# The second feed-forward layer computed row by row: gelu values as weights, w2 in quarters as moving operand

## The chip, the cores and the metric

One core of a Trainium2 chip runs one program. The metric is the device time of one execution in microseconds (us), lower is better. The kernel before takes 1184.27 us in the median of three runs (1183.27 to 1184.52). All tensors are bfloat16; matmuls accumulate in float32 in PSUM.

## The reference

A transformer block with the normalisation in front: attention with 32 heads of 32, then a feed-forward layer with gelu. There are 2048 rows of 1024 values; the hidden width is 3584.

```python
def _A_ref(x, wqkv, wo):
    B, S, D = x.shape
    H = 32; Dh = D // H
    qkv = (x @ wqkv).reshape(B, S, 3, H, Dh).transpose(2, 0, 3, 1, 4)
    q, k, v = qkv[0], qkv[1], qkv[2]
    scores = jnp.einsum("bhqd,bhkd->bhqk", q, k) * Dh ** -0.5
    o = jnp.einsum("bhqk,bhkd->bhqd", _softmax(scores, axis=-1), v)
    return o.transpose(0, 2, 1, 3).reshape(B, S, D) @ wo

def _B_ref(x, w1, b1, w2, b2):
    h = _gelu(jnp.einsum("bsd,df->bsf", x, w1) + b1)
    return jnp.einsum("bsf,fd->bsd", h, w2) + b2

h = x + _A_ref(_layernorm(x), wqkv, wo)
out = h + _B_ref(_layernorm(h), w1, b1, w2, b2)
```

## The kernel before

**A written-out order.** The program has no loop on the chip. A planner (`Plan`) records each instruction with an estimated cost and with what it reads and writes, works out the semaphore waits, and keeps for every engine one list in order. Within an engine nothing is reordered later, and a waiting instruction holds up all that stands behind it on its engine. SP issues all loads and stores, in one list too.

**Chunks.** The rows go in four chunks of 512 (`CH`). Attention is worked through in 512 units `u` (four chunks, eight groups `g` of four heads, two halves of 256 queries, eight pairs of key tiles). Each unit makes scores of four heads with 8 matmuls whose weights have 32 rows (`qk`, L1131), two exponentials of 128x1024 on ScalarE (L1140), and later the matmuls with the values and the row sums (`pv`, L1216). The scores use six PSUM banks as three pairs, bank 6 takes the values' sums, and bank 7 is the only bank (`fbanks.items = [7]`) for all other matmuls of that stage.

**Filler.** All that isn't attention is written as generators that stop (`yield Need(...)`) before each step, and the planner puts steps between scores and values when TensorE has room: first the projections of keys, queries and values (`fill0`), then, beside attention of chunk `c`, the output projection, normalisation and feed-forward of chunk `c - 1` (`ffn(ci, False)`). The test for room is `t + turn + step <= due`, where `step` is the cost of one matmul step of 512 columns, `due` is 220 ns after the scores' banks are expected to be free, and `turn` is 95 ns if scores came just before. Filler matmuls there go as quads: `wide(..., quad=True)` makes four matmuls with 32 columns of weights each, at four column positions of the array, which the array does side by side. The planner counts a quad as its columns/2.4 + 2.5 ns, and 105 ns more where the kind of matmul changes (`kind`: "R" for scores, "C" for quads and values, "F" for whole-width ones).

**The feed-forward part of `ffn`.** After `hnT` (the normalised rows, transposed) the first layer makes 28 groups `fc` of 128 hidden units; each is 8 matmuls of 512 columns, an eviction, and gelu. While attention runs, gelu is a chain of VectorE steps and a tanh on ScalarE (L1460 to L1463, two groups at a time); in the tail it is one ScalarE instruction (L1445). The results stand in `gT`, hidden units by rows. The second layer takes 8 blocks `db` of 128 output columns: weights are `w2` (128 hidden by 128 output columns), the moving operand is `gT` with 512 rows, so 28 matmuls of 512 columns make a block of the *transposed* result. VectorE (L1488), in the tail ScalarE (L1485), adds `b2`, one value for each partition, on the way into `oT`. After four blocks, four transposes for each tile of 128 rows turn the result back (`transposes`, L506 as quads, L511 whole), VectorE adds the residual rows `hch` (L1495) and the store is put on SP.

**Loads of weights.** `w1` has two slots of 512 KB (`load_w1`), `w2` two slots of 896 KB (`load_w2`, one block each, asked for one block ahead; the first two are asked for six groups before the first layer's end). `hnT`, and later `oT`, stand at `hn_off`; `x3` and later the output staging `ost` at `x3_off`.

**The tail.** After the last exponential the chunk 3 (`ffn(3, True)`) runs with nothing beside it: whole-width matmuls (`tiled[0] = False`), eight banks once the filler of chunk 2 is done, six slots for `w1` and three for `w2` in the space of the keys and values.

Of the kernel before, what the change touches and what calls it, by code (L numbers as in the profile page):

```python
# [7 lines left out]
dt = mybir.dt  # L8
# [5 lines left out]
P = 128  # L14
# [221 lines left out]
def build_kernel(nc, A_x, A_wqkv, A_wo, B_w1, B_b1, B_w2, B_b2, out):  # L236
# [100 lines left out]
    ones_pp, (B_ones,) = sb("ones_pp", [P, P], dt.bfloat16)  # L337
    ones32, (B_ones32,) = sb("ones32", [P, 32], dt.bfloat16)
    blk, (B_blk,) = sb("blk", [P, 32], dt.bfloat16)
    b2bf, (Bf_b2bf,) = sb("b2bf", [P, DC], dt.bfloat16)  # L340
    b2f, (Bf_b2f,) = sb("b2f", [P, DC], dt.float32)
    b1bf, (Bf_b1bf,) = sb("b1bf", [P, FC], dt.bfloat16)
    b1f, (Bf_b1f,) = sb("b1f", [P, FC], dt.float32)
    biasm, _ = sb("biasm", [P, G, NCH], dt.float32)
# [584 lines left out]
    with_b = [("b1", b1bf, B_b1, Bf_b1bf), ("b2", b2bf, B_b2, Bf_b2bf)]  # L929
    for _, t_, src, B_ in with_b:  # L930
        dma(t_[:], src.rearrange("(c p) -> p c", p=P), 8192, writes=[B_], lanes=lanes_a, noncontig=True)
    pool(lambda g: g.tensor_copy(b1f[:], b1bf[:]), reads=[Bf_b1bf], writes=[Bf_b1f])
    pool(lambda g: g.tensor_copy(b2f[:], b2bf[:]), reads=[Bf_b2bf], writes=[Bf_b2f])


    PT, B_PTf = sb("PT", [P, NPU, 4, 512], dt.bfloat16, nbufs(NPU * 2), at=late_off)
# [320 lines left out]
    def ffn_alloc():  # L1257
        cursor[0] = region0
        f = ffn_bufs

        def area(name, nbytes):
            f[name] = cursor[0]
            cursor[0] += nbytes

        area("g_off", FC * 1024)
        area("hn_off", DC * 1024)
        area("x3_off", 4 * 2048)
        f["w1"], f["B_w1"] = sb("w1", [P, 2, DC, 256], dt.bfloat16, nbufs(2))
        f["w2_off"] = cursor[0]
        f["w2"], f["B_w2"] = sb("w2", [P, 2, FC, P], dt.bfloat16, nbufs(2))  # L1270
# [46 lines left out]
    def ffn(ci, tail):  # L1317
# [82 lines left out]
        def load_w2(db):  # L1400
            if db in w2s or db >= DC:
                return
            s = w2s[db] = n12[1] % len(B_w2_)
            n12[1] += 1
            dma(w2[:, s, :, :], B_w2[:, db * P:(db + 1) * P].rearrange("(c p) d -> p c d", p=P), FC * P * P * 2,
                writes=[B_w2_[s]], lanes=lanes_w)
# [26 lines left out]
        for bk in range(FC // 2):  # L1433
            s = w1s[bk]
            for u in range(2):
                fc = bk * 2 + u
                if u == 1:
                    load_w1(bk + len(B_w1_) - 1)
                if fc == FC - 6:
                    for db in range(len(B_w2_)):  # L1440
                        load_w2(db)
# [24 lines left out]
                yield from group([(w1[:, s, dc, u * P:(u + 1) * P], hnT[:, dc, 0:w]) for dc in range(DC)], evac,  # L1466
                                 lambda i, s=s: [B_w1_[s]] + B_hnT[:n4], n=w)
        oT, B_oT = sb(f"oT{ci}", [P, DC, 512], dt.bfloat16, nbufs(DC), at=hn_at)
        ost, B_ost = sb(f"ost{ci}", [P, 8, 512], dt.bfloat16, nbufs(8), at=x3_at)
        for hf in range(2):  # L1470
            for d4 in range(4):
                db = hf * 4 + d4
                s = w2s[db]
                bank = fbanks.next()
                quad = tiled[0]
                for fc in range(FC):
                    if fc == 6:
                        load_w2(db + len(B_w2_) - 1)
                    if fc % 2 == 0:
                        yield Need([B_gT[fc], B_gT[fc + 1], B_w2_[s]], [B_ps[bank]] if fc == 0 else [],  # L1480
                                   [g_ch[fc + 1]] if fc + 1 in g_ch else [])
                    wide(bank, 0, w, w2[:, s, fc, :], gT[:, fc, 0:w], fc == 0, fc == FC - 1,
                         [B_gT[fc], B_w2_[s]], [B_ps[bank]] if fc in (0, FC - 1) else [], fc == FC - 1, quad)
                if tail:
                    act(lambda a, bank=bank, db=db: a.activation(oT[:, db, 0:w], ps[:, bank, 0:w], ACT.Identity, bias=b2f[:, db:db + 1], scale=1.0),  # L1485
                        reads=[B_ps[bank], Bf_b2f], writes=[B_oT[db]], cost=180 + .85 * w)
                else:
                    dve(lambda v, bank=bank, db=db: v.tensor_scalar(oT[:, db, 0:w], ps[:, bank, 0:w], b2f[:, db:db + 1], None, ALU.add),  # L1488
                        reads=[B_ps[bank], Bf_b2f], writes=[B_oT[db]], cost=690)
            for t4 in range(n4):  # L1490
                bank = fbanks.next()
                yield Need(B_oT[hf * 4:hf * 4 + 4], [B_ps[bank]])
                tp = transposes(lambda k, t4=t4, hf=hf: oT[:, hf * 4 + k, t4 * P:(t4 + 1) * P], B_oT[hf * 4:hf * 4 + 4], bank, 4)
                o = hf * 4 + t4
                dve(lambda v, tp=tp, o=o, t4=t4, hf=hf: v.tensor_tensor(ost[:, o, :], tp, hch[:, t4, hf * 512:(hf + 1) * 512], ALU.add),  # L1495
                    reads=[B_ps[bank], B_hch[2 * t4 + hf]], writes=[B_ost[o]], cost=690)
                r0_ = q0 + t4 * P

                def store(r0_=r0_, hf=hf, o=o):
                    dma(out2[r0_:r0_ + P, hf * 512:(hf + 1) * 512], ost[:, o, :], 131072, reads=[B_ost[o]], lanes=lanes_o, is_out=True)  # L1500
                    if ci < NCH - 2:
                        load_rows(r0_ + 512, o % 4, hf)
# [12 lines left out]
    u = 0  # L1515
# [197 lines left out]
```

## Time and profile before

| what | value |
|---|---|
| runs | 1184.27 us median of 3 (1183.27 to 1184.52) |
| the profiled execution | 1182.17 us |
| its span, from first to last instruction | 1180.4 us |
| granted TensorE clock, mean | 0.994 |
| exponentials of attention (L1140) | 1024, 954.1 us busy, 1124 ns each |
| second layer beside attention (L529, gT and w) | 2688 matmuls of 128x512 = 672 quads, 169.0 us busy |
| second layer in the tail (L524, gT and w_t) | 224 matmuls of 128x512, 48.7 us busy |
| transposes back (L506; L511 in the tail) | 384 matmuls, 9.6 us busy; 32, 2.1 us |
| evictions with b2 (L1488 VectorE; L1485 ScalarE) | 24 of 750 ns; 8 of 687 ns |
| residual additions (L1495 VectorE) | 32 of 425 ns |
| eviction with addition from a whole bank (L1358 VectorE) | 32 of 692 ns |
| loads of w2, 896 KB: issue to landing, median | 5.9 us beside attention, 5.0 us in the tail |
| loads of w1, 512 KB | 3.7 us |

The span begins with the first instruction and ends with the last; the profiled execution's time holds some 1.8 us more around it. In rows of the timeline the columns are: start in us from the span's start, duration in us from the first start to the last end, engine, line, operation, output and inputs, weights' rows*columns and the shape, how many, and in brackets idle time before the first and what ended it. PE is TensorE, PEld its weight loads, DVE VectorE, ACT ScalarE, SPq the DMA queue of SyncE. Instructions of one engine overlap in their pipelines, so the step from start to start is shorter than the duration of one, and an engine that is "busy" throughout can still be fed late.

### The profile page before, as it was taken

What the parts mean: (1) busy time and instruction counts of PE and PEld (TensorE: products, weight loads), DVE (VectorE), ACT (ScalarE), POOL (GpSimd) and SP (SyncE); (2) the same over time, 40 slices, a digit from 0 to 9 for tenths busy, and PEclk for the clock granted to TensorE, in tenths of its full rate; (3) what the DMA queues carried; (4) which work ended last, traced back from release to release, by engine and by line L of the source; (5) the groups of instructions that cost most, each with busy time, mean ns of one, the idle gap of its engine ahead of it and who ended that gap; (6) DMA issues with size and microseconds to landing.
All of it is one profiled execution on the core that took longest, in us unless ns stands there. A gap on an engine that the chain in (4) does not pass through costs nothing.

```text
span 1180.4 us, 48866 instructions
## 1 busy us (share of the span) xinstructions
PE 1102.0 (93%) x22638; PEld 556.3 (47%) x22638; DVE 663.0 (56%) x1182; ACT 1050.8 (89%) x1157; POOL 20.1 (2%) x60
## 2 busy tenths in 40 slices
PE   6999999999998999999998999999999999997998
PEld 3646455554444444444444444444444444443443
DVE  8564565555656778444556887444667864452000
ACT  7798999899999999999999999999999999962410
POOL 2100000000000000000000000000000000000000
PEclk9999999999999999999999999999999999998999
DMA  9201000003401233442502242351012513342643
GB/s 268 46 21 39 21 3 12 12 12 92 100 12 56 84 106 77 96 101 62 144 11 74 74 127 65 79 132 57 21 56 75 153 34 96 83 145 77 177 94 99
DMA packets 231870, 91.24 MB, mean 77 GB/s; under 512 B 155376, under 2 KB 229104, under 8 KB 231664
## 3 DMA queue, kind: packets, MB, share of 16 engines
q1 hardware_dynamic: 231664, 88.10, 28.5%
q8 instruction: 177, 2.90, 1.0%
q14 instruction: 29, 0.24, 0.1%
HBM read 83.90 MB, written 4.19 MB: 75 GB/s over the span
## 4 chain that ended last, share of the span: by engine, by line
ACT 43%; PE 41%; issue 8%; DVE 5%; DMA 2%; SPq 1%; POOL 0%; POOLq 0%; DVEq 0%; ACTq 0%
ACT PT L1140 40%; PE ps L529 18%; PE ps L524 10%; PE ps L1216 6%; PE ps L1131 5%; ACT tm L1462 2%; DMA w<-in_B_w_dram 1%; PE ps L803 1%; DVE lnst L481 1%; PE ps L858 1%; DVE Rg L1229 1%; DVE gT L1448 1%; DVE QT L1231 1%; SPq L288 1%; PE ps L511 1%
## 5 line engine op out<-in xcount | busy, mean ns | idle before, releaser
L1140 ACT ACTIVATE PT<-ps 128x1024 bf16<-128x1024 f32 x1024 | 954.1, 1124 | 15.1 <-DVE biasm L681 9.7
L1216 PE MATMUL ps<-PT,V 128*32 128x256 bf16 x4096 | 227.6, 274 | 17.2 <-ACT PT L1140 11.0
L1165 DVE TENSOR_TENSOR FS<-PT 128x1024 bf16<-128x1024 bf16 x227 | 155.6, 689 | 147.3 <-ACT PT L1140 118.3
L1131 PE MATMUL ps<-QT,KT 32*128 32x256 bf16 x4096 | 203.6, 273 | 22.8 <-ACT PT L1140 18.9
L529 PE MATMUL ps<-hnT,w 128*32 128x512 bf16 x2688 | 173.0, 381 | 6.5 <-DVE gT L1448 3.9
L529 PE MATMUL ps<-gT,w 128*32 128x512 bf16 x2688 | 169.0, 380 | 0.4 <-DVE oT L1488 0.3
L1131 PEld LDWEIGHTS ps<-QT,KT 32*128 32x128 bf16 x4096 | 61.0, 92 | 196.4 <-ACT PT L1140 184.9
L1216 PE MATMUL ps<-PT,ones 128*32 128x256 bf16 x2280 | 144.0, 273 | 0.0
L1216 PEld LDWEIGHTS ps<-PT,V 128*32 128x32 bf16 x4096 | 106.2, 96 | 70.8 <-ACT PT L1140 25.2
L529 PEld LDWEIGHTS ps<-hnT,w 128*32 128x32 bf16 x2688 | 61.4, 96 | 78.0 <-issue 28.4
L1448 DVE TENSOR_SCALAR gT<-ps,b1f 128x512 bf16<-128x512 f32 x84 | 63.0, 750 | 54.9 <-PE ps L529 54.0
L529 PEld LDWEIGHTS ps<-gT,w 128*32 128x32 bf16 x2688 | 68.7, 97 | 51.5 <-issue 4.8
L1495 DVE TENSOR_TENSOR ost<-ps,hch 128x512 bf16<-128x512 bf16 x32 | 13.0, 422 | 116.5 <-PE ps L511 102.1
L1216 PEld LDWEIGHTS ps<-PT,ones 128*32 128x32 bf16 x2280 | 61.4, 97 | 10.4
L1216 PE MATMUL ps<-FS,ones 128*32 128x256 bf16 x908 | 65.2, 277 | 0.0
L529 PE MATMUL ps<-xnTe,wk 128*32 128x512 bf16 x832 | 55.6, 389 | 4.3 <-DVE kmax L646 2.3
L1463 DVE SCALAR_TENSOR_TENSOR gT<-tm,gT 128x1024 bf16<-128x1024 bf16 x42 | 51.2, 1219 | 2.7 <-ACT tm L1462 2.1
L524 PE MATMUL ps<-hnT,w_t 128*128 128x512 bf16 x224 | 50.8, 392 | 1.2 <-ACT hnT L1422 1.2
L1461 DVE SCALAR_TENSOR_TENSOR tm<-tm,gT 128x1024 bf16<-128x1024 bf16 x42 | 51.3, 1221 | 0.8
L1462 ACT ACTIVATE tm<-tm 128x1024 bf16<-128x1024 bf16 x42 | 50.3, 1197 | 0.0
L524 PE MATMUL ps<-gT,w_t 128*128 128x512 bf16 x224 | 48.7, 379 | 0.0
L1445 ACT ACTIVATE gT<-ps,b1f 128x512 bf16<-128x512 f32 x28 | 19.2, 687 | 32.5 <-PE ps L524 32.5
(135 smaller groups left out, 899.4 us busy)
## 6 DMA issues: line engine op xcount, KB each, us to landing
w<-in_B_w_dram SPq DMA_DIRECT2D x42, 512.0 KB, 3.7
w<-in_B_w_dram SPq DMA_DIRECT2D x24, 896.0 KB, 5.9
w_t<-in_B_w_dram SPq DMA_DIRECT2D x14, 512.0 KB, 3.7
w_t<-in_B_w_dram SPq DMA_DIRECT2D x8, 896.0 KB, 5.0
xr<-in_A_x_dram SPq DMA_DIRECT2D x16, 256.0 KB, 6.0
wk<-in_A_wqkv_dram SPq DMA_DIRECT2D x16, 256.0 KB, 3.1
wq<-in_A_wqkv_dram SPq DMA_DIRECT2D x16, 256.0 KB, 4.2
out_dram<-ost SPq DMA_DIRECT2D x32, 128.0 KB, 2.3
```

The lines of the kernel that those rows point to most:

```text
L524: pe(lambda p: p.matmul(ps[:, bank, lo:lo + n], lhsT, rhs, start=start, stop=stop), reads=reads, writes=writes, inc=inc, cost=mm(n))
L529: pe(lambda p, r=r: p.matmul(ps[32 * r:32 * r + 32, bank, lo:lo + n], lhsT[:, 32 * r:32 * r + 32], rhs, start=start, stop=stop, tile_posit ...
L1131: pe(lambda p, k=k, kt=kt, r=r, b=b: p.matmul(ps[:, b, k * 256:(k + 1) * 256], KT[32 * r:32 * r + 32, g, kt * P:(kt + 1) * P], QT[32 * r:3 ...
L1140: act(lambda a, safe, i=i, b=b: a.activation(PT[:, o_, 2 * i:2 * i + 2, :], ps[:, b:b + 2, :], ACT.Exp, bias=0.0 if safe else biasm[:, g, ...
L1165: dve(lambda v: v.tensor_tensor(FS[:, f_, :, :], PT[:, o_, :, 0:256], PT[:, o_, :, 256:512], ALU.add), reads=B_PT[o_], writes=[B_FS[f_]], ...
L1216: pe(lambda p, d=d, r=r, lhsT=lhsT, rhs=rhs, n=n: p.matmul(ps[32 * r:32 * r + 32, OD, d * 256:(d + 1) * 256], lhsT, rhs, start=(start and ...
L1445: act(lambda a: a.activation(gT[:, fc, 0:w], ps[:, bank, 0:w], ACT.Gelu_apprx_tanh, bias=b1f[:, fc:fc + 1], scale=1.0), reads=[B_ps[bank], ...
L1448: dve(lambda v: v.tensor_scalar(gT[:, fc, 0:w], ps[:, bank, 0:w], b1f[:, fc:fc + 1], 0.5, ALU.add, ALU.mult), reads=[B_ps[bank], Bf_b1f], ...
L1461: (E.DVE, lambda v: v.scalar_tensor_tensor(t_, t_, GB, x_, ALU.add, ALU.mult), [Bt] + Bx, [Bt], 1220),
L1462: (E.Activation, lambda a: a.activation(t_, t_, ACT.Tanh, scale=GK), [Bt], [Bt], 946),
L1463: (E.DVE, lambda v: v.scalar_tensor_tensor(x_, t_, 1.0, x_, ALU.add, ALU.mult), [Bt] + Bx, Bx, 1220)])
L1495: dve(lambda v, tp=tp, o=o, t4=t4, hf=hf: v.tensor_tensor(ost[:, o, :], tp, hch[:, t4, hf * 512:(hf + 1) * 512], ALU.add), reads=[B_ps[ban ...
```

## The change

The operands of the second layer change places. For each quarter `q` of 256 output columns and each tile of 128 rows, 28 matmuls take `gT` (128 hidden units by 128 rows) as weights and a quarter of `w2` (128 hidden by 256 columns) as moving operand, so that rows of the result come out untransposed. Two tiles share a PSUM bank. After the 28 comes one more matmul which adds `b2`: its weights are four rows, of which only row `q` is one, and its moving operand is `b2` as four rows of 256. One VectorE addition of the residual takes the whole bank to `ost`, and one store takes two tiles by 256 columns to memory. `oT`, its evictions, the transposes back and the column-wise `b2` go.

`w2` is loaded by quarters, each as two loads of 14 groups of 128 hidden units (two of 896 KB, rows of 256 values in place of 128). Quarter 0 is asked for where the first two blocks were, quarter 1 when the first layer has been recorded, quarters 2 and 3 when the quarter two before has been. Even quarters use the place of the old two slots, odd ones the place of `hnT` and of most of `w1`; `x3_off` moves in front of `hn_off` so that those lie side by side. In the tail both places are in the space of the values, `w1` has four slots in place of six, and `x3` and `hnT` move into the space of the keys.

```diff
-    b2bf, (Bf_b2bf,) = sb("b2bf", [P, DC], dt.bfloat16)
-    b2f, (Bf_b2f,) = sb("b2f", [P, DC], dt.float32)
+    b2row, (B_b2row,) = sb("b2row", [4, 256], dt.bfloat16)
...
+    dma(b2row[:], B_b2.rearrange("(a c) -> a c", a=4), 2048, writes=[B_b2row], lanes=lanes_a)
...
-        area("hn_off", DC * 1024)
         area("x3_off", 4 * 2048)
+        area("hn_off", DC * 1024)
+        f["w1_off"] = cursor[0]
...
-            f["w1"], f["B_w1"] = sb("w1_t", [P, 6, DC, 256], dt.bfloat16, nbufs(6), at=k2_off)
-            f["w2"], f["B_w2"] = sb("w2_t", [P, 3, FC, P], dt.bfloat16, nbufs(3), at=v_off)
+            f["w1"], f["B_w1"] = sb("w1_t", [P, 4, DC, 256], dt.bfloat16, nbufs(4), at=k2_off)
...
+        def load_w2(q, part=None):
+            if q not in w2s:
+                at = (v_off + q % 2 * 14336 if tail else f["hn_off"] if q % 2 else f["w2_off"])
+                w2s[q] = sb(f"w2_{ci}_{q}", [P, 2, FC // 2, 256], dt.bfloat16, nbufs(2), at=at)
+            w2, B = w2s[q]
+            for h in range(2):
+                if part in (None, h):
+                    dma(w2[:, h, :, :], B_w2[h * FC * 64:(h + 1) * FC * 64, q * 256:(q + 1) * 256].rearrange("(c p) d -> p c d", p=P), FC * P * 256,
+                        writes=[B[h]], lanes=lanes_w)
...
-        for hf in range(2):
-            for d4 in range(4):
-                db = hf * 4 + d4
...
-                    wide(bank, 0, w, w2[:, s, fc, :], gT[:, fc, 0:w], fc == 0, fc == FC - 1,
-                         [B_gT[fc], B_w2_[s]], [B_ps[bank]] if fc in (0, FC - 1) else [], fc == FC - 1, quad)
...
+        load_w2(1)
+        for q in range(4):
+            w2, B_w2_ = w2s[q]
+            for t in range(0, n4, 2):
+                bank = fbanks.next()
+                quad = tiled[0]
+                for u in range(2):
+                    lo = (t + u) * P
+                    for fc in range(FC):
+                        if fc % 2 == 0:
+                            yield Need([B_gT[fc], B_gT[fc + 1], B_w2_[fc // (FC // 2)]], [B_ps[bank]] if u == 0 and fc == 0 else [],
+                                       [g_ch[fc + 1]] if fc + 1 in g_ch else [])
+                        wide(bank, u * 256, 256, gT[:, fc, lo:lo + P], w2[:, fc // (FC // 2), fc % (FC // 2), :], fc == 0, False,
+                             [B_gT[fc], B_w2_[fc // (FC // 2)]], [B_ps[bank]] if fc == 0 else [], False, quad)
+                    wide(bank, u * 256, 256, ident[0:4, q:q + 1].to_broadcast([4, P]), b2row[:], False, True,
+                         [B_ident, B_b2row], [B_ps[bank]], True, quad)
+                o = q * 2 + t // 2
+                dve(lambda v, o=o, t=t, q=q, bank=bank: v.tensor_tensor(
+                    ost[:, o, :, :], ps[:, bank, :].rearrange("p (u c) -> p u c", u=2), hch[:, t:t + 2, q * 256:(q + 1) * 256], ALU.add),
+                    reads=[B_ps[bank]] + [B_hch[2 * (t + u) + q // 2] for u in range(2)], writes=[B_ost[o]], cost=690)
...
+                def store(r0_=r0_, q=q, o=o, t=t):
+                    dma(out2[r0_:r0_ + 2 * P, q * 256:(q + 1) * 256].rearrange("(u p) c -> p u c", p=P), ost[:, o, :, :], 131072,
+                        reads=[B_ost[o]], lanes=lanes_o, is_out=True)
...
+            if q < 2:
+                load_w2(q + 2)
```

More of the change, by code (lines that the diff above doesn't have):

```diff
@@ L928, in build_kernel @@
     v_left = [proj_v(2 * p, 0, "act") for p in range(NT // 2) if ("V", p) in jobs]
-    with_b = [("b1", b1bf, B_b1, Bf_b1bf), ("b2", b2bf, B_b2, Bf_b2bf)]
-    for _, t_, src, B_ in with_b:
-        dma(t_[:], src.rearrange("(c p) -> p c", p=P), 8192, writes=[B_], lanes=lanes_a, noncontig=True)
+    dma(b1bf[:], B_b1.rearrange("(c p) -> p c", p=P), 8192, writes=[Bf_b1bf], lanes=lanes_a, noncontig=True)
+    dma(b2row[:], B_b2.rearrange("(a c) -> a c", a=4), 2048, writes=[B_b2row], lanes=lanes_a)
     pool(lambda g: g.tensor_copy(b1f[:], b1bf[:]), reads=[Bf_b1bf], writes=[Bf_b1f])
-    pool(lambda g: g.tensor_copy(b2f[:], b2bf[:]), reads=[Bf_b2bf], writes=[Bf_b2f])
     PT, B_PTf = sb("PT", [P, NPU, 4, 512], dt.bfloat16, nbufs(NPU * 2), at=late_off)
@@ L1265, in ffn_alloc @@
         area("g_off", FC * 1024)
+        area("x3_off", 4 * 2048)
         area("hn_off", DC * 1024)
-        area("x3_off", 4 * 2048)
+        f["w1_off"] = cursor[0]
         f["w1"], f["B_w1"] = sb("w1", [P, 2, DC, 256], dt.bfloat16, nbufs(2))
         f["w2_off"] = cursor[0]
-        f["w2"], f["B_w2"] = sb("w2", [P, 2, FC, P], dt.bfloat16, nbufs(2))
+        f["w2"], f["B_w2"] = sb("w2", [P, 2, FC // 2, 256], dt.bfloat16, nbufs(2))
         f["NG"] = 3
@@ L1325, in ffn @@
         if tail:
-            f["w1"], f["B_w1"] = sb("w1_t", [P, 6, DC, 256], dt.bfloat16, nbufs(6), at=k2_off)
-            f["w2"], f["B_w2"] = sb("w2_t", [P, 3, FC, P], dt.bfloat16, nbufs(3), at=v_off)
-        w1, w2, tm = f["w1"], f["w2"], f["tm"]
+            f["w1"], f["B_w1"] = sb("w1_t", [P, 4, DC, 256], dt.bfloat16, nbufs(4), at=k2_off)
+        w1, tm = f["w1"], f["tm"]
         B_tm_ = f["B_tm"]
-        B_w1_, B_w2_, NG = f["B_w1"], f["B_w2"], f["NG"]
-        hc_at, x3_at, hn_at = (qt_off, k2_off + 24576, v_off + 21504) if tail else (hch_off, f["x3_off"], f["hn_off"])
+        B_w1_, NG = f["B_w1"], f["NG"]
+        hc_at, x3_at, hn_at = (qt_off, k2_off + 16384, k2_off + 24576) if tail else (hch_off, f["x3_off"], f["hn_off"])
         n12 = [0, 0] if tail else f["n12"]
@@ L1398, in load_w1 @@
                 writes=[B_w1_[s]], lanes=lanes_w)
[L1400 to L1406, printed above, removed]
+        def load_w2(q, part=None):
[7 more added lines that the diff above has]
+                        writes=[B[h]], lanes=lanes_w)
         for bk in range(len(B_w1_)):
@@ L1439, in ffn @@
                 if fc == FC - 6:
-                    for db in range(len(B_w2_)):
-                        load_w2(db)
+                    load_w2(0)
                 def evac(bank, fc=fc):
@@ L1467, in ffn @@
                                  lambda i, s=s: [B_w1_[s]] + B_hnT[:n4], n=w)
-        oT, B_oT = sb(f"oT{ci}", [P, DC, 512], dt.bfloat16, nbufs(DC), at=hn_at)
-        ost, B_ost = sb(f"ost{ci}", [P, 8, 512], dt.bfloat16, nbufs(8), at=x3_at)
-        for hf in range(2):
-            for d4 in range(4):
-                db = hf * 4 + d4
-                s = w2s[db]
+        ost, B_ost = sb(f"ost{ci}", [P, 8, 2, 256], dt.bfloat16, nbufs(8), at=x3_at)
+        load_w2(1)
+        for q in range(4):
+            w2, B_w2_ = w2s[q]
+            for t in range(0, n4, 2):
@@ L1474, in ffn @@
                 bank = fbanks.next()
                 quad = tiled[0]
[L1476 to L1481, printed above, removed]
-                    wide(bank, 0, w, w2[:, s, fc, :], gT[:, fc, 0:w], fc == 0, fc == FC - 1,
-                         [B_gT[fc], B_w2_[s]], [B_ps[bank]] if fc in (0, FC - 1) else [], fc == FC - 1, quad)
@@ L1484, in ffn @@
[L1484 to L1502, printed above, removed]
-                stores.append(chain([("call", store, [B_ost[o]], [], 0)]))
+                for u in range(2):
[8 more added lines that the diff above has]
+                         [B_ident, B_b2row], [B_ps[bank]], True, quad)
@@ new lines, in ffn @@
+                o = q * 2 + t // 2
+                dve(lambda v, o=o, t=t, q=q, bank=bank: v.tensor_tensor(
+                    ost[:, o, :, :], ps[:, bank, :].rearrange("p (u c) -> p u c", u=2), hch[:, t:t + 2, q * 256:(q + 1) * 256], ALU.add),
+                    reads=[B_ps[bank]] + [B_hch[2 * (t + u) + q // 2] for u in range(2)], writes=[B_ost[o]], cost=690)
+                r0_ = q0 + t * P
+                def store(r0_=r0_, q=q, o=o, t=t):
+                    dma(out2[r0_:r0_ + 2 * P, q * 256:(q + 1) * 256].rearrange("(u p) c -> p u c", p=P), ost[:, o, :, :], 131072,
+                        reads=[B_ost[o]], lanes=lanes_o, is_out=True)
+                    if ci < NCH - 2 and q % 2:
+                        for u in range(2):
+                            load_rows(r0_ + 512 + u * P, t + u, q // 2)
@@ L1504, in ffn @@
+                stores.append(chain([("call", store, [B_ost[o]], [], 0)]))
+            if q < 2:
+                load_w2(q + 2)
+        if not tail:
+            for k, q in ((0, 3), (1, 2)):
+                lo, B = (f["w1_off"], B_w1_) if q == 3 else (f["w2_off"], f["B_w2"])
+                plan.track(lo, lo + (8192 if q == 3 else 14336), B)
         marks.add(("ffn", ci))
```

## The prediction

> **What bounds the kernel now.** I read the page first: the span, the engine shares and the forty slices.
>
> ```profile
> span 1180.4 us, 48866 instructions
> PE 1102.0 (93%) x22638; PEld 556.3 (47%) x22638; DVE 663.0 (56%) x1182; ACT 1050.8 (89%) x1157; POOL 20.1 (2%) x60
> ...
> PE   6999999999998999999998999999999999997998
> ...
> ACT  7798999899999999999999999999999999962410
> ...
> ACT 43%; PE 41%; issue 8%; DVE 5%; DMA 2%; SPq 1%; POOL 0%; POOLq 0%; DVEq 0%; ACTq 0%
> ```
>
> The reader is to see two regimes. Up to slice 35 ScalarE and TensorE are both full (attention, with the feed-forward of the chunk before as filler); then ScalarE empties and TensorE alone carries the tail, the fourth chunk. So a price has to be asked twice: what does it do to ScalarE's row of exponentials, and what to TensorE's row in the tail? ScalarE first, in the timeline of its engine:
>
> ```profile
> 819.36 43.19 ACT L1140 ACTIVATE PT<-ps 128x1024 bf16<-128x1024 f32 x47
> ...
> 956.88 93.08 ACT L1140 ACTIVATE PT<-ps 128x1024 bf16<-128x1024 f32 x100
> ...
> 959.82 4.73 ACT L1140 ACTIVATE PT<-ps 128x1024 bf16<-128x1024 f32 x5
> ```
>
> One exponential lasts 1.124 us (page), but they overlap. The five at 959.82 follow each other at (4.73 - 1.124)/4 = 0.902 us: the rate of an undisturbed ScalarE. The hundred from 956.88, beside the second layer of chunk 2, need (93.08 - 1.124)/99 = 0.929; the 47 from 819.36, beside the output projection, whose filler steps are single quads of 512 columns, 0.915. So "busy" hides some 0.027 x 99 = 2.7 us of lateness in a second-layer stage: scores that come late hold ScalarE up, and TensorE's order decides it. Then TensorE:
>
> ```profile
> 96.12 1.93 PE L529 MATMUL ps<-wv,xnTl 128*32 128x256 bf16 x64
> ...
> 1034.10 0.40 PE L1131 MATMUL ps<-QT,KT 32*128 32x256 bf16 x8
> 1034.42 1.91 PE L529 MATMUL ps<-gT,w 128*32 128x512 bf16 x32
> 1036.27 0.40 PE L1131 MATMUL ps<-QT,KT 32*128 32x256 bf16 x8
> ...
> 45.41 1.91 PE L858 MATMUL ps<-wv,xnTl 128*128 128x256 bf16 x16
> 47.25 0.40 PE L830 MATMUL ps<-sqk,blk 128*32 128x512 bf16 x4
> 47.58 1.92 PE L858 MATMUL ps<-wv,xnTl 128*128 128x256 bf16 x16
> ```
>
> Four matmuls of 32 columns of weights go side by side as a quad. Eight quads of 512 in 1.91 us, less the last one's 0.379 and 0.012 between its four starts: 0.217 us each. Sixteen quads of 256 in 1.93: (1.93 - 0.273 - 0.012)/15 = 0.110. Whole-width matmuls of 256: (1.91 - 0.273)/15 = 0.109. The third and fourth rows show the price of changing the division of the array: the last 512-quad starts at 1034.42 + 7 x 0.217 = 1035.94, the scores 0.33 later instead of 0.217; back again the second score quad starts at 1034.22, the next filler 0.20 later instead of 0.11. So 0.1 us each way, 0.2 for a visit. The last three rows say the same of whole width against quads (47.05 to 47.25, 47.47 to 47.58). Last the tail:
>
> ```profile
> 1124.24 24.34 PE L524 MATMUL ps<-gT,w_t 128*128 128x512 bf16 x112
> ...
> 1149.35 1.07 PE L511 MATMUL ps<-ident,oT 128*128 128x128 bf16 x16 [0.78 <-ACT oT L1485]
> ...
> 1150.26 24.34 PE L524 MATMUL ps<-gT,w_t 128*128 128x512 bf16 x112
> ...
> 1174.63 0.69 ACT L1485 ACTIVATE oT<-ps,b2f 128x512 bf16<-128x512 f32 x1 [5.36 <-PE ps L524]
> 1175.37 0.90 PEld L511 LDWEIGHTS ps<-ident,oT 128*128 128x128 bf16 x16 [1.27 <-ACT oT L1485]
> ...
> 1175.81 1.42 DVE L1495 TENSOR_TENSOR ost<-ps,hch 128x512 bf16<-128x512 bf16 x4 [24.60 <-PE ps L511]
> 1176.26 2.22 SPq L288 DMA_DIRECT2D out_dram<-ost  x4
> ```
>
> Matmuls of 512 run at (24.34 - 0.380)/111 = 0.216 us; between the halves, and after the second, an eviction, transposes and additions stand bare.
>
> **The tail, term by term.** (1) 448 matmuls of 256 at 0.1091 replace 224 of 512 at 0.2159: 48.88 - 48.36 = +0.5 us. The doubled weight loads (98 ns) hide, as in the L858 rows, which load 128x128 weights before each 256. (2) 16 bias matmuls at 0.109: +1.7. (3) The gap between the halves goes: the next matmul could have started at 1148.42 and did at 1150.26: -1.8. (4) The end: from the last matmul's end (1174.60) to the span's end at 1180.37 were 5.8 us. Now follow one addition of 128x512 from PSUM (0.69 by the L1358 rows, the same shape), a hop of 0.06, and one store: 1.7 (the shortest landing) to 2.3 (the median), say 1.9, and about 0.45 to the end as before: 3.1, so -2.7; the last matmul is 0.1 shorter, -0.1. Without anything else: -2.4. (5) Does a bias matmul, of four rows, cost a change of division? No row of the trace has fewer than 32 rows. Below: nothing, for quads of 32 columns stay quads of 32 columns. Above: a visit each, 16 x 0.2 = 3.2, less the way back of the last, 3.1. I take the upper: the scores, whose weights have 32 rows, do pay, and a matmul's division seems to be taken from its operands' rows and columns. Tail: **+0.7 us**.
>
> The Trainium skill, TensorEngine Tiling (Array Packing), Key Properties, says that changing the tiling mode drains TensorE, while changing the tile does not. By it four rows belong to a 32-row mode, and the tail is the +0.7; read so that four rows stay in the 128-row mode it is -2.4. The rows above agree with the drain at 0.1 us a side for 32 rows; none shows four.
>
> **The attention stage.** TensorE per chunk: 448 x 0.110 - 224 x 0.217 = +0.7 us, 16 bias quads +1.8, their visits 0 to +3.2, eight transposes gone (16 matmuls at 0.056 a quad, 0.23 each) -1.8; and 8 handovers of the only filler bank in place of 16. At worst +3.9 a chunk, 11.7 for three. As mere work this is hidden: the last second-layer matmul starts at 1041.6, the exponentials end at 1049.98, and from 1066 to 1070 in the tail TensorE does nothing; with the cover gone, each us would lengthen the tail by one. VectorE's 8 evictions of 0.75 and 8 additions of 0.425 become 8 of 0.69: -3.9 us a chunk on an engine 56% busy, nothing. What is not hidden is lateness of scores, in two opposite terms.
> (6) The planner tests room for one quad of 512 but then records a pair of them, 0.43 us; a pair of 256 is 0.22 and fits the test. If the second layer's exponentials come at the 0.915 of the projection instead of 0.929, over some 100 in each of three stages: -4.2; below that nothing, since TensorE may simply use the time otherwise. I take half, **-2.1**.
> (7) The planner books a bias quad without a visit (its kind is "C", like its neighbours), so real scores come up to 0.2 later than planned, 48 times: 0 to 48 x 0.2 = +9.6. Some of it is eaten: TensorE waits for ScalarE before scores 56 times for 18.9 us (view of waits), 0.3 each, spread over the whole program, and every second bias quad is followed by a bank handover, in which TensorE waits anyway. I take a third, **+3.2**.
> (8) Gelu: the last pair is ready at 957.25 + 1.23 = 958.5, the first pass began at 953.11 and reached that pair near 961. At half the columns it gets there near 956.3 and pauses 2.2 us a chunk; the pending values are taken first. Filler, not scores: 0, at worst 3 x 2.2 in the cover above.
> (9) DMA. Quarters are loaded as two of 896 KB; such loads land after 5.9 us (in the tail 5.0). Quarter 1 lies over hnT and w1 and so is asked for at the end of the first layer, needed a quarter later (22 us as filler, 12.7 in the tail); quarters 2 and 3 wait on SP for the end of the quarter two before. Two in a row: 10 to 12 us, hidden; 12.7 - 10.0 leaves 2.7 in the tail. Behind these waits on SP stand only stores of a finished pair, whose eight slots no one takes again in the chunk, and in chunks 0 and 1 rows for the next. The tail's w1 goes from six slots to four: still three blocks of 3.45 us ahead of a landing of 3.7.
>
> Sum: +0.7 - 2.1 + 3.2 = **+1.8 us**. The profiled execution took 1182.17 us around its span of 1180.4, so 1184.0 there; the runs' median is 1184.27, and I give the forecast on it: **1186.1**.
>
> **Rivals.** (A) The forecast, 0.44; its own range, from terms 6 and 7, 1183.5 to 1190. (B) Four rows cost no visit: tail -2.4, filler -2.1, -4.5: **1179.8**. For it: the quads' columns stay; against: what the 32-row scores pay. 0.22. (C) Nothing absorbs the visits and the finer steps bring nothing: each bias quad pushes the next scores out by 0.2: +9.6 + 0.7: **1194.6**. For it: TensorE is at 9 in every slice; against: its waits for ScalarE. 0.19. (D) Visits are paid but absorbed, the finer steps bring all: -4.2 + 0.7: **1180.8**. For it: 0.915 beside single quads; against: that stage has other filler. 0.15. Slower begins for certain where term 7 exceeds term 6 by 1.7.
>
> Less than 0.2% (2.4 us) can't be told from no change here. Faster: 0.20 of B, 0.10 of D: 0.30. Slower: C's 0.18 and 0.24 of A's upper part: 0.42. Same: 0.28. The range 1180 to 1192 leaves out the far ends of B and C, about 0.2.
>
> **What would show it.** The bias rows: 0.2 us more than 0.11 from their neighbours (A, C, D) or not (B). The mean step of exponentials beside the second layer: above 0.929 C, near it A, 0.915 D. The tail from the second layer's first matmul to the end: 56.8 us with visits, 53.7 without, where it was 56.1. Wrong altogether would be a wait for w2 in the tail, or second-layer work left after the last exponential.

## The result and the profile after

The changed kernel takes 1200.48 us in the median of four runs (1198.61 to 1203.81); the kernel before took 1183.77 (1182.13 to 1184.52) beside it. The ratio is 1.0145, with a 95% interval of 1.0126 to 1.0164: the change costs 16 to 17 us. Forecast were 1186.1, with 1192 as the upper end. The page of the changed kernel:

```profile
span 1196.8 us, 54116 instructions
...
PE 1116.4 (93%) x25263; PEld 642.4 (54%) x25274; DVE 666.9 (56%) x1175; ACT 1047.3 (88%) x1149; POOL 20.3 (2%) x59
...
PE   6999999999998999999999999989899999998998
...
ACT  7798999899999999999999999999999999962400
...
q8 instruction: 198, 3.24, 1.1%
...
L1137 ACT ACTIVATE PT<-ps 128x1024 bf16<-128x1024 f32 x1024 | 955.6, 1110 | 27.9 <-PE ps L1128 16.6
...
L528 PE MATMUL ps<-w,gT 128*32 128x256 bf16 x5376 | 178.6, 273 | 5.4 <-issue 4.9
```

The span grew by 16.4 us. VectorE lost its evictions into `oT`, but its busy time went from 663.0 to 666.9 us: the planner now gives it 244 sums of exponentials of 689 ns (L1162) where it had 227. Three things are new. ScalarE's idle time before exponentials (L1137, which was L1140) is 27.9 us, of which 16.6 end with late scores. In the kernel before it was 15.1 and 3.8, by the page and by the view of waits:

```profile
L1140 ACT ACTIVATE PT<-ps 128x1024 bf16<-128x1024 f32 x1024 | 954.1, 1124 | 15.1 <-DVE biasm L681 9.7
...
ACT PT L1140 <- PE ps L1131: 3.8, 6, 1.2
```

The second layer's matmuls (L528, which was L529) have idle time that ends in "issue": TensorE stood with nothing to wait for that the trace shows. And the program has 5250 more instructions; the queue that brings instructions (q8) made 198 packets where it made 177.

Where in the span? The last exponential ends at 1065.43, before at 1049.97: attention lost 15.5 us, the tail 1.0 (131.4 after 130.4). Not all of the 15.5 stands beside the second layer, whose first matmul starts at 463.21 before and at 466.66 after. The exponentials around these two points, the same ones of each program:

```profile
461.24 5.76 ACT L1140 ACTIVATE PT<-ps 128x1024 bf16<-128x1024 f32 x6
464.69 5.64 ACT L1137 ACTIVATE PT<-ps 128x1024 bf16<-128x1024 f32 x6
```

So 3.45 us had been lost before any matmul of the second layer ran. From 52 to 463 us the granted clock was 1.00 in the kernel before and 0.98 in this execution of the changed one; it was 1.00 in both beside the second layer. The other 12.0 us are lost from there on, and ScalarE's timeline shows their form. This is the changed kernel beside the second layer of chunk 2:

```profile
972.02 23.95 ACT L1137 ACTIVATE PT<-ps 128x1024 bf16<-128x1024 f32 x26 [0.83 <-PE ps L1128]
997.15 25.83 ACT L1137 ACTIVATE PT<-ps 128x1024 bf16<-128x1024 f32 x28 [1.19 <-PE ps L1128]
1024.23 14.79 ACT L1137 ACTIVATE PT<-ps 128x1024 bf16<-128x1024 f32 x16 [1.25 <-PE ps L1128]
1039.30 14.84 ACT L1137 ACTIVATE PT<-ps 128x1024 bf16<-128x1024 f32 x16 [0.27 <-PE ps L1128]
1054.29 11.14 ACT L1137 ACTIVATE PT<-ps 128x1024 bf16<-128x1024 f32 x12 [0.15 <-PE ps L1128]
```

Within a row the step is good: (25.83 - 1.110)/27 = 0.916 us, better than the 0.929 of before. The rows are cut by gaps, the longest of 1.19 and 1.25 us; over all 98 the step is (1065.43 - 972.02 - 1.110)/97 = 0.952. It is not a steady slowing but some events. The view of TensorE's waits in the changed kernel has them (engine, line and releaser; then total us, times, longest):

```profile
PE ps L528 <- issue: 4.9, 5, 1.6
...
PE ps L1213 <- issue: 3.5, 2, 2.4
...
PE ps L1128 <- issue: 1.2, 1, 1.2
```

These are 9.6 us beside attention, in eight halts; the kernel before has no such row for TensorE. TensorE's timeline around one of them:

```profile
498.04 0.40 PE L1128 MATMUL ps<-QT,KT 32*128 32x256 bf16 x8
...
498.70 0.49 PE L528 MATMUL ps<-w,gT 128*32 128x256 bf16 x10
500.59 1.05 PE L528 MATMUL ps<-w,gT 128*32 128x256 bf16 x30 [1.39 <-issue]
501.57 0.40 PE L1128 MATMUL ps<-QT,KT 32*128 32x256 bf16 x8
```

A run of quads, all of whose operands have long been there, breaks off after ten matmuls, in the middle of the third quad, and goes on 1.39 us later. The scores behind it come 3.5 us after the scores before, and an exponential is late by it. The large halts begin at 499.2, 521.8, 758.7, 785.4, 995.3 and 1022.6 us: two in each of the three chunks, each 6 to 8 us after the first load of a pair of w2 loads was issued. The trace's DMA records beside the first:

```
instruction packets (q8, 16 KB each), start:  486.51  490.78  498.09  501.90  505.75
the two w2 loads, issue to landing:           490.96 to 496.22,  491.37 to 499.23
TensorE stands:                               499.20 to 500.59
```

A packet of 16 KB is due every 4 us here. While the two loads run, none starts for 7.3 us, and at the end of that gap TensorE stands. The size fits: by the page (3.24 + 0.24 MB)/54116 is 64 bytes for an instruction, so a packet holds some 256; a quad of 256 columns is eight instructions (four weight loads, four matmuls) in 0.110 us, and at that rate a packet lasts 3.5 us. This suggested a theory: **a pair of loads back to back keeps the instruction packets waiting, and halved matmuls eat up the instructions in hand before the next arrives.** Its rivals: the visits of the bias rows push the scores (rival C of the prediction), and the halved matmuls alone are at fault, whatever is loaded.

### The profile page after: what moved, and what is told of

It reads as the page before. It is cut to its first block, busy times and chain, and to the rows that moved or that the text cites. A ratio compares the mean times of both kernels' runs of the same rounds, so it can differ in the third digit from the quotient of the medians.

```text
span 1196.8 us, 54116 instructions
## 1 busy us (share of the span) xinstructions
PE 1116.4 (93%) x25263; PEld 642.4 (54%) x25274; DVE 666.9 (56%) x1175; ACT 1047.3 (88%) x1149; POOL 20.3 (2%) x59
## 3 DMA queue, kind: packets, MB, share of 16 engines
q8 instruction: 198, 3.24, 1.1%
## 4 chain that ended last, share of the span: by engine, by line
ACT 45%; PE 40%; issue 9%; DVE 5%; DMA 0%; POOL 0%; POOLq 0%; ACTq 0%; DVEq 0%
ACT PT L1137 41%; PE ps L528 16%; PE ps L523 10%; PE ps L1213 7%; PE ps L1128 5%; ACT tm L1460 3%; DVE lnst L480 1%; PE ps L802 1%; DVE Rg L1226 1%; DVE Rg L1224 1%; PE ps L857 1%; DVE QT L1228 1%; PE ps L510 0%; DVE gT L1446 0%; DVE gT L1461 0%
## 5 line engine op out<-in xcount | busy, mean ns | idle before, releaser
L1137 ACT ACTIVATE PT<-ps 128x1024 bf16<-128x1024 f32 x1024 | 955.6, 1110 | 27.9 <-PE ps L1128 16.6
L1162 DVE TENSOR_TENSOR FS<-PT 128x1024 bf16<-128x1024 bf16 x244 | 167.2, 689 | 160.9 <-ACT PT L1137 127.6
L528 PE MATMUL ps<-w,gT 128*32 128x256 bf16 x5376 | 178.6, 273 | 5.4 <-issue 4.9
L528 PE MATMUL ps<-hnT,w 128*32 128x512 bf16 x2688 | 173.3, 381 | 5.5 <-DVE gT L1446 4.0
L528 PEld LDWEIGHTS ps<-w,gT 128*32 128x32 bf16 x5376 | 135.7, 97 | 26.4 <-issue 18.6
L1213 PE MATMUL ps<-PT,ones 128*32 128x256 bf16 x2144 | 137.1, 274 | 0.0
L528 PEld LDWEIGHTS ps<-hnT,w 128*32 128x32 bf16 x2688 | 61.6, 96 | 76.7 <-issue 27.5
L1484 DVE TENSOR_TENSOR ost<-ps,hch 128x512 bf16<-128x512 f32 x32 | 22.1, 690 | 123.1 <-PE ps L523 100.6
L1213 PE MATMUL ps<-FS,ones 128*32 128x256 bf16 x976 | 70.1, 277 | 0.3 <-DVE FS L1162 0.2
L1213 PEld LDWEIGHTS ps<-PT,ones 128*32 128x32 bf16 x2144 | 57.7, 97 | 10.9
L528 PE MATMUL ps<-xnTe,wk 128*32 128x512 bf16 x832 | 57.3, 399 | 4.3 <-DVE kmax L645 2.3
L523 PE MATMUL ps<-w,gT 128*128 128x256 bf16 x448 | 51.7, 273 | 0.0
L1460 ACT ACTIVATE tm<-tm 128x1024 bf16<-128x1024 bf16 x42 | 50.1, 1192 | 0.0
```

The source lines that it names most:

```text
L523: pe(lambda p: p.matmul(ps[:, bank, lo:lo + n], lhsT, rhs, start=start, stop=stop), reads=reads, writes=writes, inc=inc, cost=mm(n))
L528: pe(lambda p, r=r: p.matmul(ps[32 * r:32 * r + 32, bank, lo:lo + n], lhsT[:, 32 * r:32 * r + 32], rhs, start=start, stop=stop, tile_posit ...
L1137: act(lambda a, safe, i=i, b=b: a.activation(PT[:, o_, 2 * i:2 * i + 2, :], ps[:, b:b + 2, :], ACT.Exp, bias=0.0 if safe else biasm[:, g, ...
L1162: dve(lambda v: v.tensor_tensor(FS[:, f_, :, :], PT[:, o_, :, 0:256], PT[:, o_, :, 256:512], ALU.add), reads=B_PT[o_], writes=[B_FS[f_]], ...
L1213: pe(lambda p, d=d, r=r, lhsT=lhsT, rhs=rhs, n=n: p.matmul(ps[32 * r:32 * r + 32, OD, d * 256:(d + 1) * 256], lhsT, rhs, start=(start and ...
L1484: dve(lambda v, o=o, t=t, q=q, bank=bank: v.tensor_tensor(ost[:, o, :, :], ps[:, bank, :].rearrange("p (u c) -> p u c", u=2), hch[:, t:t + ...
```

## The experiments

In the table "last exp" is the end of the last exponential, "tail" what follows it to the span's end, and "issue" the idle time of TensorE beside attention that ends in "issue", from the view of waits; all in us from the profiled execution. "From" is the start of the first matmul of the second layer beside attention; up to there TensorE has the same work in all of them. The ratio is to the kernel before on the same chip.

| kernel | median us | ratio, 95% interval | from | last exp | tail | issue |
|---|---|---|---|---|---|---|
| before | 1181.80 to 1183.77 | 1 | 463.21 | 1049.97 | 130.4 | 0 |
| after | 1200.48 | 1.0145 [1.0126, 1.0164] | 466.66 | 1065.43 | 131.4 | 9.6 |
| e1_split | 1197.44 | 1.0121 [1.0104, 1.0138] | 463.82 | 1067.0 | 131.6 | 8.4 |
| e2_bias128 | 1195.08 | 1.0104 [1.0081, 1.0127] | 466.54 | 1066.0 | 127.7 | 12.4 |
| e3_both | 1191.91 | 1.008 [1.0062, 1.0098] | 463.72 | 1060.98 | 128.2 | 11.8 |
| e4_before256 | 1189.73 | 1.0051 [1.0032, 1.0071] | 466.23 | 1058.68 | 130.0 | 4.4 |
| e5_paced | 1178.25 | 0.9964 [0.995, 0.9978] | 464.10 | 1047.76 | 128.3 | 0 |
| e6_noload | 1179.24 | 0.9976 [0.996, 0.9991] | 463.13 | 1047.92 | 127.9 | 1.1 |
| e7_half | 1179.07 | 0.9972 [0.9959, 0.9986] | 463.07 | 1049.08 | 128.4 | 0.6 |
| e8_paced4 | 1186.52 | 1.0036 [1.0022, 1.005] | 463.81 | 1053.14 | 131.7 | 0 |

**The two halves of a quarter apart.** Beside attention the second load of each quarter is asked for later than the first; in the first chunk they are 12 to 16 us apart.

```diff
-        load_w2(1)
+        load_w2(1, None if tail else 0)
...
+                if not tail and t == 0 and q < 3:
+                    load_w2(q + 1, 1, [B_ost[o]])
...
-                load_w2(q + 2)
+                load_w2(q + 2, None if tail else 0)
```

> The changed kernel, with the two loads of a quarter taken apart beside attention: the first half as before, the second half only when half of the quarter in front of it is done (some 11 us later). Same matmuls, same bytes. Theory F (fetch): the halts of TensorE in the second layer (six of 1.4 to 2.5 us that end in 'issue', eight late exponentials of 0.9 to 2.2 us, 13 us together) come from its instructions being fetched behind two 896 KB loads in a row. Then those halts go, and the time falls by 10 to 13 us, to 1187 to 1191; no gap between two 16 KB instruction packets over 6 us in the second layer. Theory V (visits): the bias quads' visits, 48 of 0.2 us, and other lateness push the scores out. Then nothing changes: 1200. Theory W (w2 comes late): the time rises, since half of a quarter now comes later.

It was 1197.44; the intervals of its ratio and of the changed kernel's, 1.0121 and 1.0145, overlap. The halts became more and shorter, eleven where there were eight, seven of them 0.7 to 1.7 us long; their sum fell only from 9.6 to 8.4. The last exponential came no sooner, but in this execution the granted clock was 0.96 and 0.98 in the first two chunks' second layers, where the changed kernel had 1.00, so a part of its lateness is the clock's. It is not the pair alone: each halt begins 5.6 to 7.5 us after a single load of 896 KB was issued. What moved is where they stand, which ties them to the loads.

**The bias with 128 rows.** The weights of the bias matmul become a whole identity column, with b2 in the first four of 128 rows and zeros below, so that no matmul has fewer than 128 rows.

```diff
-    b2row, (B_b2row,) = sb("b2row", [4, 256], dt.bfloat16)
+    b2row, (B_b2row,) = sb("b2row", [P, 256], dt.bfloat16)
+    pool(lambda g: g.memset(b2row[:], 0.0), writes=[B_b2row])
...
-    wide(bank, u * 256, 256, ident[0:4, q:q + 1].to_broadcast([4, P]), b2row[:], False, True,
+    wide(bank, u * 256, 256, ident[:, q:q + 1].to_broadcast([P, P]), b2row[:], False, True,
```

> The changed kernel, with b2 held in 128 rows of which 124 are zero, and a whole column of the identity as weights, so that the bias matmul has 128 rows like its neighbours. Under F and V alike the visits go: the tail falls by 3.1 us. Beside attention, F expects 0 to 3 us more (1194 to 1198 in all), V expects 48 x 0.2 = 9.6 more (about 1188). That a bias quad follows its neighbour after 0.11 us and not 0.2 would show that the rows of the operands set the division of the array.

The tail's second layer, from its first matmul to the end, shrank from 57.0 to 53.85 us: the 16 visits were worth 3.2, or 0.2 each. The last exponential did not move (1066.0 after 1065.4), and the halts grew to 12.4; the granted clock was 0.98 in the second layers of the second and third chunk. So what the visits cost beside attention can't be read from this kernel.

**Both together.**

> Both edits. F expects 1182 to 1187: the halts gone and the tail 2.1 us shorter than in the kernel before (1184). V expects the same as with 128 rows of bias alone.

1191.91, about the sum of the two gains. The last exponential comes 4.5 us sooner than in the changed kernel, but 2.9 of these were gained before the second layer began; from its first matmul on it takes 597.3 us, where the changed kernel takes 598.8 and the kernel before 586.8. There are still thirteen halts of 0.2 to 1.6 us, 11.8 in all, and 10.5 us of the loss beside attention are left.

**The kernel before with halved matmuls.** Nothing of the change but its finer matmuls: each quad of 512 columns of the old second layer beside attention is written as two of 256. The loads stay as they were, one of 896 KB at a time, with rows of 128 values.

```diff
-                    wide(bank, 0, w, w2[:, s, fc, :], gT[:, fc, 0:w], fc == 0, fc == FC - 1,
-                         [B_gT[fc], B_w2_[s]], [B_ps[bank]] if fc in (0, FC - 1) else [], fc == FC - 1, quad)
+                    for c in ((0, 256) if quad else (0,)):
+                        n = 256 if quad else w
+                        wide(bank, c, n, w2[:, s, fc, :], gT[:, fc, c:c + n], fc == 0, fc == FC - 1,
+                             [B_gT[fc], B_w2_[s]], [B_ps[bank]] if fc in (0, FC - 1) else [], fc == FC - 1, quad)
```

> The kernel before, with each 512-column quad of the second layer beside attention written as two quads of 256 columns (the same weights twice): 2688 more matmuls and weight loads, as in the changed kernel, with single 896 KB loads at the old places. Streaming grows by 224 x 3 x 0.003 = 2 us of filler. F expects little: a single load holds the fetch up for some 3 us, 0 to 5 us, 1184 to 1189, with few halts over 0.9 us. If twice the instructions alone were the cause, it should lose the 13 us: 1197.

1189.73, +0.5%. The last exponential is 8.7 us later; 3.0 of these had been lost before the second layer began, and 5.7 come after, with nine halts of 4.4 us in all, the longest 0.8. So the extra instructions cost time beside the old loads too, about half as much as the 12.0 of the changed kernel.

**Paced loads.** With the 128-row bias, each quarter comes as seven loads of 256 KB, one for every 16 quads of the quarter before (quarter 0 with the last seven groups of the first layer). The tail keeps its halves.

```diff
+                        tick = nbufs(1) if not tail and q < 3 and step % (4 * 4) == 0 else []
+                        wide(bank, u * 256, 256, gT[:, fc, lo:lo + P], w2[:, fc, :], fc == 0, False,
+                             [B_gT[fc], B_w2_[fc // 2]], ([B_ps[bank]] if fc == 0 else []) + tick, bool(tick), quad)
+                        if tick:
+                            load_w2(q + 1, step // (4 * 4) * 4, 4, tick)
+                        step += 1
```

> The changed kernel with 128 rows of bias and, beside attention, each quarter of w2 in seven loads of 256 KB, one after every 16 matmul steps of the quarter in front of it (quarter 0: one after each of the last seven groups of the first layer). Same bytes, same matmuls, no load over 0.8 us of transfer. Theory F (instructions are fetched behind w2's packets): the halts in 'issue' go almost wholly, the exponentials end near 1051 us as in the kernel before, and with a second layer of 53.9 us in the tail instead of 56.1 the time is 1179 to 1184. Theory N (so many instructions are slow whatever is loaded): as with two spread halves, 1190 to 1193.

1178.25: faster than both kernels. It has the matmuls and the bytes of the bias-128 kernel, and no halt. ScalarE's timeline, to set beside the five rows of the changed kernel above:

```profile
957.37 79.14 ACT L1138 ACTIVATE PT<-ps 128x1024 bf16<-128x1024 f32 x86 [0.84 <-PE ps L1129]
1036.65 11.11 ACT L1138 ACTIVATE PT<-ps 128x1024 bf16<-128x1024 f32 x12 [0.15 <-PE ps L1129]
```

Eighty-six in one row, at (79.14 - 1.11)/85 = 0.918. Its list of DMA issues, median from issue to landing last:

```profile
w<-in_B_w_dram SPq DMA_DIRECT2D x84, 256.0 KB, 2.8
```

In the changed kernel the 32 loads of 896 KB landed after 7.9. Here, in the first chunk, the packets of instructions started at 487.53, 492.07, 496.49, 501.03 and 504.60, evenly, between such loads.

**No loads.** As in the bias-128 kernel, but beside attention only quarter 0 of w2 is loaded, and used for the other three.

```diff
             for h in range(2):
                 if part in (None, h):
+                    if q and not tail:
+                        continue
...
-            w2, B_w2_ = w2s[q]
+            w2, B_w2_ = w2s[q if tail else 0]
```

> The changed kernel with 128 rows of bias; beside attention only quarter 0 of w2 is loaded and stands in for the other three (what is left out: their loads, so the values of chunks 0 to 2 are not the reference's). Same instructions on TensorE. F: halts only near quarter 0's load, the rest gone, 1178 to 1184. N: as with the loads, about 1195.

1179.24, and the last exponential at 1047.92, within 0.2 us of the paced kernel. Against the bias-128 kernel the ratio falls from 1.0104 to 0.9976, some 15 us, which is about all of that kernel's loss beside attention: it hangs on the loads, and the same bytes in small, spread loads cost nothing. Whether small loads in a row would do as well, no run shows. The one halt that is left, 1.15 us at 699.1, stands in a first layer, behind loads of `w1` and of quarter 0.

**Half the instructions.** As in the bias-128 kernel with its pairs of 896 KB loads, but one quad of 512 columns stands for two quads of 256: the same columns through TensorE with half the instructions.

```diff
+                        if quad:
+                            if fc % 2 == 0:
+                                wide(bank, 0, 512, gT[:, fc, lo:lo + P], w2[:, fc // (FC // 2), fc % (FC // 2):fc % (FC // 2) + 2, :].rearrange("p a b -> p (a b)"), u == 0 and fc == 0, False,
+                                     [B_gT[fc], B_w2_[fc // (FC // 2)]], [B_ps[bank]] if fc == 0 else [], False, quad)
+                            continue
```

> The changed kernel with 128 rows of bias and its pairs of 896 KB loads, but beside attention each two quads of 256 columns are one quad of 512, taking both groups' columns of w2 with the first group's gelu values (what is changed: chunks 0 to 2 get other values; streaming, loads and waits stay). Half the instructions. F, with both parts needed: TensorE uses up its store of instructions half as fast and lasts through a pair of loads, halts go or fall under a third, 1179 to 1185. If the pair of loads alone were enough: 1192 to 1196.

1179.07, with two halts of 0.6 us in all, both in first layers. This is the sharpest pair of views. Stretches of 2 us of the changed kernel, while its pair of loads of 490.96 runs (busy us of TensorE, its weight loads, VectorE, ScalarE and GpSimd, each with its count; then the granted clock, the DMA share and GB/s):

```profile
494.00:496.00 2.00, 2.00 (x76) 1.52 (x64) 0.00 (x0) 2.00 (x4) 0.00 (x0) 1.00 1.16 311
496.00:498.00 2.00, 2.00 (x68) 1.30 (x56) 0.69 (x1) 2.00 (x3) 0.00 (x0) 1.00 1.19 293
498.00:500.00 2.00, 1.20 (x34) 0.66 (x31) 0.69 (x1) 2.00 (x3) 0.00 (x0) 1.00 0.51 125
500.00:502.00 2.00, 1.41 (x42) 0.98 (x45) 0.00 (x0) 0.62 (x1) 0.00 (x0) 1.00 0.03 8
```

And of the kernel with half the instructions, whose pair was issued at 485.43 and 485.84:

```profile
488.00:490.00 2.00, 2.00 (x48) 0.99 (x44) 0.57 (x1) 2.00 (x3) 0.00 (x0) 1.00 1.18 307
490.00:492.00 2.00, 2.00 (x52) 0.99 (x44) 0.46 (x1) 2.00 (x3) 0.00 (x0) 1.00 1.17 292
492.00:494.00 2.00, 2.00 (x48) 0.99 (x44) 0.86 (x2) 2.00 (x3) 0.00 (x0) 1.00 0.81 200
494.00:496.00 2.00, 2.00 (x48) 0.80 (x36) 0.79 (x4) 2.00 (x4) 0.00 (x0) 1.00 0.03 4
```

The same loads at the same 300 GB/s, the clock at 1.00 in both. With 76 matmuls in 2 us TensorE falls to 34 as the loads end; with 48 it runs on. The packets' gap is even longer here, 484.34 to 492.84 us, without a halt: at 48 matmuls in 2 us the instructions in hand last longer than at 76. That the loads slow the matmuls while they run is not borne out: the changed kernel has 76 matmuls from 494 to 496 us at 311 GB/s, and 76 from 488 to 490 with no transfer at all. The halt comes after.

**Paced loads, bias with four rows.** The paced kernel with the change's own bias matmul, which leaves only the visits.

> The paced kernel, with the changed kernel's bias of four rows put back: the visits alone, without halts. In the tail 16 visits cost 3.2 us (57.0 against 53.9 from the second layer's first matmul, as the runs so far have it). Beside attention, 48 visits: all pushed on to the scores 9.6 us, all absorbed 0; the forecast took a third, 3.2. So 1178.3 + 3.2 + (0 to 9.6), that is 1181 to 1191; by the forecast's third 1184.7. Paced with 128 rows runs beside it in an earlier call, so the ratios to the kernel before are compared.

1186.52, no halts. Against the paced kernel the last exponential is 1053.14 - 1047.76 = 5.4 us later and the tail's second layer 57.07 - 53.85 = 3.2 us longer. This is the price of the visits without halts; the granted clock in the first chunk's second layer was 0.98 in this execution and 1.00 in the paced one, and by an estimate of 0.02 of 97 us up to 2 of the 5.4 can be that. ScalarE shows them as a step of (64.83 - 1.11)/69 = 0.924 in the row that answers to the 0.918:

```profile
961.92 64.83 ACT L1137 ACTIVATE PT<-ps 128x1024 bf16<-128x1024 f32 x70 [0.84 <-PE ps L1128]
```

**Whose packets were late.** The records of all these runs answer it together. The queue q8 made 177 packets in the kernel before, 198 in the changed one and 177 in the kernel with half the instructions; at 256 instructions each that is 45312, 50688 and 45312. TensorE's matmuls and weight loads are 45276, 50537 and 45169 by the pages. So q8 brings TensorE's instructions and next to nothing else. Beside attention seven of the ten kernels have halts of TensorE that end in "issue", 53 in all. Counted in TensorE's recorded instructions from the start of the program, each of the 53 falls at the same place of a block of 256: at 189 in the three kernels whose trace lacks some matmul records, at 193 in the four that lack none. TensorE stops only where one packet ends and the next begins. And each halt ends 2.2 to 2.9 us after the start of the packet that closed a gap of 5.1 to 9.6 us, as 500.59 - 498.09 = 2.50 above. TensorE stood because its next packet of instructions came late.

## Why the prediction was wrong

By the ratios, taken of 1182 us, the change costs 17.1: -4.3 from before to the paced kernel (2.1 of it in the tail), +8.5 for the visits (3.2 in the tail), +12.9 for the halts. In the other order it is -4.3, +16.5 for the halts alone, and the visits then +4.8. By the intervals each step is uncertain by 2 to 3 us. The profiled executions, from the first matmul of the second layer to the last exponential, say much the same: 586.8 us before, 583.7 paced, 589.3 with the visits, 598.8 with the halts too, which is -3.1, +5.7 and +9.4. In either order the halts are most of it. That the visits seem to cost less where there are halts would fit a TensorE that is held up elsewhere anyway, but the difference is within the uncertainty.

**Where it failed: term 9.** "Two in a row: 10 to 12 us, hidden." The loads did land in time for their use (8.3 us from the first issue of the pair to the second landing at 499.23). But the term asked of a load only when it lands, not what it delays on its way. And the matmuls were costed by TensorE's time, 0.110 against half of 0.217, while "the doubled weight loads hide" took no account of what 5250 more instructions ask of the queue that delivers them. Where the sum had nothing, the runs show 9.6 us of halts in the profile and 12.9 us by the ratios. Each half was harmless: pairs of loads with quads of 512 (half the instructions) 0.9972, quads of 256 with no or small loads 0.9976 and 0.9964. Together they are 1.0104, and none of the forecast's terms stood for that. The page of before had a line for it, `q8 instruction: 177, 2.90, 1.0%`, which I passed over as 1% of a resource.

What is shown is that the second layer's halts need both the instructions and the large loads, and go when either goes, and that they stand where TensorE's next packet is late. What holds the packet up while the loads run, the records don't tell.

**Term 7, the visits beside attention.** Forecast +3.2, within 0 to 9.6; measured 8.5 - 3.2 = 5.3 by the ratios and 5.7 by the profiles. The mechanism and its bounds were right; whether a third of it or a half comes through, these runs don't decide.

**Term 6, the finer steps.** Forecast -2.1, within 0 to -4.2; measured -4.3 + 2.1 = -2.2 by the ratios and -3.1 by the profiles, in the paced kernel, with a step of 0.918 where 0.929 was before and 0.915 was hoped for. The mechanism was right; that half of the most came out is partly luck, for the half was chosen without a row to show it.

**Term 5, rival B.** Four rows do pay. The quads' rows of the changed kernel, in the order of the timeline:

```profile
1048.15 0.40 PE L528 MATMUL ps<-w,gT 128*32 128x256 bf16 x8
1048.48 0.10 PEld L528 LDWEIGHTS ps<-b2row,ident 4*32 4x32 bf16 x4 [0.21 <-issue]
1048.48 0.29 PE L528 MATMUL ps<-b2row,ident 4*32 4x256 bf16 x4
1048.70 0.62 PE L528 MATMUL ps<-w,gT 128*32 128x256 bf16 x16
```

Two quads and a bias quad would take 0.33; the next starts after 0.55. Without the visit the kernel is what B had forecast, and near its 1179.8: the paced kernel at 1178.25 (0.9964), whose gain is of B's size in both parts: some 2 us in attention and 2.1 in the tail.

**Terms 1 to 5, the tail.** Forecast +0.7, measured +1.0. The tail of the changed kernel:

```profile
1139.76 3.22 PE L523 MATMUL ps<-w,gT 128*128 128x256 bf16 x28
1142.90 0.09 PEld L523 LDWEIGHTS ps<-b2row,ident 4*128 4x128 bf16 x1 [0.21 <-issue]
1142.91 0.28 PE L523 MATMUL ps<-b2row,ident 4*128 4x256 bf16 x1
1143.12 3.23 PE L523 MATMUL ps<-w,gT 128*128 128x256 bf16 x28
...
1193.51 0.28 PE L523 MATMUL ps<-b2row,ident 4*128 4x256 bf16 x1
1193.83 0.69 DVE L1484 TENSOR_TENSOR ost<-ps,hch 128x512 bf16<-128x512 f32 x1 [6.05 <-PE ps L523]
1194.54 0.37 SPq L288 DMA_DIRECT2D out_dram<-ost  x1
```

Each pass lasts 1143.12 - 1139.76 = 3.36 us, where 28 x 0.109 + 0.109 + 0.2 gives 3.36. The second layer takes 57.0 us with visits and 53.9 without; forecast were 56.8 and 53.7. From the last matmul's end (1193.79) to the span's end there are 3.0 us, forecast 3.1. No gelu and no w2 is waited for (term 8 and the tail of term 9). Second-layer work was left after the last exponential, which the prediction called a sign of being wrong altogether: 15 quads, from 1080.84 to 1082.78. They lay in TensorE's wait for the normalisation, which still ended with 3.83 us of idle time after them: hidden, as the cover was meant to be.

The prediction's own sign, a mean step above 0.929, came true (0.952) and would have pointed to C. It was the wrong reading: a mean can't tell a price paid 48 times from eight halts. The single rows can.

## What to carry to other kernels

When a matmul is halved, ask what its instructions cost to deliver, and which large loads run at that time: pairs of 896 KB loads with twice the instructions cost 13 to 16 us here, while the same bytes in loads of 256 KB, spread over their time, cost nothing. Idle time of TensorE that ends in "issue", up to 2.5 us long and beginning some 6 to 8 us after a large load was issued, is the sign. And a bias by matmul should have as many rows as its neighbours: zeros below the four rows cost no time and saved 0.2 us at every visit of the tail.

## What the runs showed of the hardware

TensorE's instructions come in packets of 16 KB, of 256 instructions, about 4 us apart in this stage; under two 896 KB loads at 300 GB/s no packet started for 6.7 to 8.0 us at the six large halts of the changed kernel, and for 7.7 to 10 us at the loads of the kernel with half the instructions. At eight instructions per 0.110 us a gap of 7.3 us ended in a halt of 1.4 us; at eight per 0.217 us gaps of 8.5 and 10 us did not. The first layer's quads of 512 are not safe from it either: between attention's quads of 256, gaps of 9.4 to 9.6 us ended in halts of 0.25 to 1.15 us (kernels with half the instructions and with no loads). The Trainium skill, Runtime: NRT & Kernel Launch, section Instruction fetch mechanics, says that each sequencer fetches blocks of 256 instructions over a DMA queue of its own while it works off the block before, and that crossing a block is mostly hidden. The packets of 16 KB, the queue that brings TensorE's alone and the halts at the blocks' borders agree with it; "mostly hidden" does not hold in this kernel, where eight halts came to 9.6 us.

A matmul with four rows costs a change of the array's division against neighbours with 128 rows, 0.1 us each way, both for quads and at whole width (the rows above); with 128 rows, most of them zero, a pass of the tail starts 3.17 us after the one before (1122.21 and 1125.38 in the paced kernel), which is 29 x 0.109, so the bias costs its 0.109 us and no more. The Trainium skill, TensorEngine Tiling (Array Packing), Key Properties, has the drain at a change of mode, and these rows agree.
